# One scaled V copy, longer P and Z buffer rows and a remade order in a gated mix of softmax and linear attention

## The chip, the core and the metric

The kernel runs on 1 core of one Trainium2 chip. The metric is the device time of one execution in microseconds, the median over the runs; lower is better. Engines are called by their names: TensorE (PE in the profile), VectorE (DVE), ScalarE (ACT), GpSimd (POOL) and SyncE (SP, which issues the DMAs).

## The reference

Both attentions work on the same `x` (2048 rows of 512, bf16) with 32 heads of 16 columns. The result is a gated mix of the two.

```python
def _A_ref(x, wqkv, wo):                      # softmax attention
    ...                                       # q, k, v: 32 heads of 16
    scores = jnp.einsum("bhqd,bhkd->bhqk", q, k) * (Dh ** -0.5)
    p = _softmax(scores, axis=-1)
    o = jnp.einsum("bhqk,bhkd->bhqd", p, v)
    return o.transpose(0, 2, 1, 3).reshape(B, S, D) @ wo

def _B_ref(x, wqkv, wo):                      # linear attention
    phi = lambda t: jnp.where(t > 0, t + 1, jnp.exp(t)) + 1e-6
    pq, pk = phi(q), phi(k)
    kv = jnp.einsum("bhsd,bhse->bhde", pk, v)
    z = jnp.einsum("bhsd->bhd", pk)
    num = jnp.einsum("bhqd,bhde->bhqe", pq, kv)
    den = jnp.einsum("bhqd,bhd->bhq", pq, z)[..., None] + 1e-6
    return (num / den).transpose(0, 2, 1, 3).reshape(B, S, D) @ wo

g = _sigmoid((x * gate_w).sum(-1, keepdims=True))
return g * _A_ref(x, A_wqkv, A_wo) + (1 - g) * _B_ref(x, B_wqkv, B_wo)
```

## The kernel before

**Units.** The softmax attention is cut into 2048 units: one head, 128 keys (a key block), 512 queries (a query chunk). The 32 heads are taken as four groups `t8` of eight heads; in a round, four heads (one parity of a group) are at work at once, one on each quarter of the TensorE array. There are 32 rounds of 64 units. The scores of a unit are one matmul of `Qz` and `KT` (`ps<-Qz,KT`), written to one of eight PSUM banks.

**Two ways to an exponential.** Pairs of units go to ScalarE, which takes the exponential of two banks in one instruction (`P<-ps`, 128x1024, L1141) and writes two of the `NP` P buffers. The other units go to VectorE, which computes the exponential by its bits: it adds a constant and writes an integer that, read as bf16, is a piecewise linear power of two (`Z<-ps`, L1089 for one unit, L1053 for a pair). GpSimd then adds two integer constants (`SHIFTS`) to it (`INT64_ADD`, L1115), which gives two more such terms. The sum of the `NTERM` = 3 terms, with weights `WTS`, follows the power of two closely. The three results fill three of the `NZ` Z buffers, each of which holds two units.

**Product with V.** The weights aren't applied to the terms: each term is multiplied by a V that carries its weight. `Vp` holds V with a column of ones (for the softmax's sum); `Vs` holds V times the weight, made by VectorE in `t_vs` (L1420) from `Vp`, for two groups of heads at a time. So a unit of ScalarE brings one matmul (`ps<-P,Vp`), and a unit of VectorE three (`ps<-Z,Vp` for the first term, `ps<-Z,Vs` for the others). Four such matmuls, of four heads, run side by side and add up in the round's accumulating bank. The last two rounds have them cut in halves of 256 queries. When a round is done VectorE transposes and normalises it.

**All other work** is spread between the units as tasks: the projections to K, Q and V, the linear attention (phi, its K-V product, its denominators), the gate and the last projection with the output rows (`t_final`, L1645 writes an output row block to one of two `outt` buffers, from which a DMA takes it to memory). A task takes a PSUM bank, has its matmuls, and frees the bank after VectorE or ScalarE has read it.

**What sets the order.** The program holds a planner that runs when the kernel is built. It keeps a clock for each engine with a cost for each instruction, always picks the engine that can start first, and there the candidate with the best start and priority: scores (`cand_s`), VectorE's first term (`cand_op1`), shifts (`cand_shift`), ScalarE's exponentials (`cand_exp`), products with V (`cand_pv`) and the tasks. The streams that it lays out are fixed; on the chip each engine runs its own stream and waits on semaphores. How many units go to VectorE comes out of that: `cand_s` builds a step of scores with two banks for ScalarE and, where banks are free and

```python
zok = len(z_free()) >= z_need() + NTERM and len(full) < X("DMX")
```

holds, one or two for VectorE. The planner's thresholds `X(...)` are read from a table `PLAN`, by the number of units issued so far divided by 8, with `DEF` for what an entry leaves out.

Of the kernel before, what the change touches and what calls it, by code (L numbers as in the profile page):

```python
# [8 lines left out]
ALU = mybir.AluOpType  # L9
# [136 lines left out]
def bass_gated_mix__mha_block__linear_attn_block__prompt_kernel(  # L146
# [19 lines left out]
    SHIFTS = (0, 42, 85)  # L166
    WTS = (1.0, 0.79296875, 0.63671875)

    def spl(t):
# [277 lines left out]
    with ExitStack() as es:  # L447
# [36 lines left out]
        OAT = SB([128, NT8, S], BF16, "OAT")  # L484
# [519 lines left out]
        def v_res(t8, w, kb):  # L1004
            return r_Vp[t8][kb // 2] if w == 0 else r_Vs[t8 % 2][w - 1][kb // 4]
# [943 lines left out]
```

## Time and profile before

| | |
|---|---|
| median of 3 runs | 625.99 us |
| lowest, highest | 625.38, 626.42 us |
| span of the profiled execution | 624.3 us |
| the profiled execution's own time | not listed apart from its span |
| busy: TensorE, VectorE, ScalarE, GpSimd | 616.6, 596.5, 610.2, 470.5 us |
| granted TensorE clock | 1.000 |

The span goes from the first to the last instruction. Busy time counts an instruction from its start to the end of its record; records of one engine overlap by some tens of nanoseconds or more, so that the time which one of them occupies is better read from start to start in the timeline. In the groups by line, L639 is a helper through which nearly all matmuls go; there the names of the operands tell the work apart.

### The profile page before, as it was taken

How to read it: one execution, taken by the hardware profiler on the slowest of the kernel's cores; microseconds unless marked ns; L12 is line 12 of the kernel's file. 1: busy time of each engine (PE TensorE's matmuls, PEld its weight loads, DVE VectorE, ACT ScalarE, POOL GpSimd, SP SyncE). 2: the span in 40 equal slices, each digit the busy share in tenths (PEclk: the TensorE clock that was granted, in tenths of full speed). 3: DMA queues.
4: the chain of work that ended last, by engine and by line, in shares of the span. 5: the costliest groups of instructions: out<-in, count | busy, mean ns of one | idle time of the engine just before them, and what ended most of it. 6: DMA issues, size and time to landing. Idle time of an engine off the chain costs nothing.

```text
span 624.3 us, 19695 instructions
## 1 busy us (share of the span) xinstructions
PE 616.6 (99%) x8432; PEld 188.9 (30%) x8432; DVE 596.5 (96%) x941; ACT 610.2 (98%) x682; POOL 470.5 (75%) x802
## 2 busy tenths in 40 slices
PE   8999999999999999999999999999999999999997
PEld 5432322433222232332222222222222222222343
DVE  6999999999999999999999999999999999999995
ACT  5999999999999999999999999999999999999996
POOL 3577687677687889866867687767799788987893
PEclk9999999999999999999999999999999999999999
DMA  6711003001110010111101011121100102010101
GB/s 145 200 43 22 14 1 54 2 2 28 36 25 4 9 27 3 19 44 26 51 8 23 26 41 24 38 50 52 28 9 17 29 11 35 3 18 27 19 11 36
DMA packets 68367, 19.64 MB, mean 31 GB/s; under 512 B 56500, under 2 KB 68148, under 8 KB 68280
## 3 DMA queue, kind: packets, MB, share of 16 engines
q1 hardware_dynamic: 67464, 17.99, 13.3%
q8 instruction: 66, 1.08, 0.7%
q10 hardware_dynamic: 816, 0.39, 0.2%
q14 instruction: 21, 0.17, 0.1%
HBM read 8.92 MB, written 4.46 MB: 21 GB/s over the span
## 4 chain that ended last, share of the span: by engine, by line
ACT 78%; PE 21%; issue 0%; POOL 0%; POOLq 0%
ACT P L1141 76%; PE ps L639 20%; ACT eb L1495 2%; PE ps L1288 0%; PE ps L1344 0%; ACT P L1643 0%; POOL warm L709 0%; ACT KT L1320 0%; POOLq L1934 0%
## 5 line engine op out<-in xcount | busy, mean ns | idle before, releaser
L1141 ACT ACTIVATE P<-ps 128x1024 bf16<-128x1024 f32 x642 | 597.4, 1138 | 3.0 <-PE ps L639 2.8
L1115 POOL INT64_ADD Z<-Z x784 | 465.3, 611 | 142.6 <-DVE Z L1089 103.9
L1089 DVE TENSOR_SCALAR Z<-ps 128x512 int16<-128x512 f32 x534 | 348.2, 680 | 11.0 <-PE ps L639 8.8
L639 PE MATMUL ps<-Qz,KT 32*128 32x512 bf16 x2048 | 255.4, 384 | 3.1 <-ACT P L1141 1.6
L639 PE MATMUL ps<-Z,Vs 128*17 128x512 bf16 (+1 forms) x1620 | 249.6, 370 | 0.1
L639 PE MATMUL ps<-P,Vp 128*17 128x512 bf16 (+1 forms) x1366 | 236.6, 369 | 0.0
L639 PE MATMUL ps<-Z,Vp 128*17 128x512 bf16 (+1 forms) x810 | 188.4, 370 | 0.0
L1053 DVE TENSOR_SCALAR Z<-ps 128x1024 int16<-128x1024 f32 x115 | 139.8, 1216 | 3.4 <-PE ps L639 1.4
L639 PEld LDWEIGHTS ps<-Qz,KT 32*128 32x128 bf16 x2048 | 66.3, 90 | 249.7 <-ACT P L1141 210.3
L639 PEld LDWEIGHTS ps<-Z,Vs 128*17 128x17 bf16 x1620 | 59.0, 89 | 47.5 <-issue 34.9
L639 PEld LDWEIGHTS ps<-P,Vp 128*17 128x17 bf16 x1366 | 54.9, 89 | 51.8 <-issue 47.1
L639 PEld LDWEIGHTS ps<-Z,Vp 128*17 128x17 bf16 x810 | 44.7, 88 | 21.8 <-issue 15.2
L639 PE MATMUL ps<-xT,wA 128*32 128x512 bf16 (+2 forms) x560 | 37.5, 369 | 0.0
L1448 DVE STREAM_TRANSPOSE T<-ps 128x512 f32<-128x512 f32 x32 | 22.6, 707 | 3.4 <-PE ps L639 3.4
L1495 ACT ACTIVATE eb<-ps 128x512 bf16<-128x512 f32 x32 | 22.3, 698 | 0.0
L1497 DVE SCALAR_TENSOR_TENSOR phiK<-ps,eb 128x512 bf16<-128x512 f32 x32 | 21.8, 680 | 0.2
L639 PE MATMUL ps<-wB,OAT 128*32 128x512 bf16 x256 | 20.4, 384 | 0.0
L639 PE MATMUL ps<-wA,xT 128*32 128x256 bf16 x512 | 20.1, 275 | 0.0
L639 PE MATMUL ps<-wB,phiK 128*32 128x512 bf16 x256 | 19.3, 382 | 0.0
L639 PE MATMUL ps<-phiK,xnat 128*32 128x512 bf16 x256 | 18.6, 383 | 0.0
L639 PE MATMUL ps<-xT,wB 128*32 128x512 bf16 x256 | 17.8, 382 | 0.0
L639 PE MATMUL ps<-wB,xT 128*32 128x512 bf16 x256 | 17.4, 381 | 0.0
(81 smaller groups left out, 193.2 us busy)
## 6 DMA issues: line engine op xcount, KB each, us to landing
xnat<-rcpd SPq DMA_DIRECT2D x16, 128.0 KB
Qz<-QT SPq DMA_DIRECT2D x120, 16.0 KB, 1.8
oad<-T SPq DMA_DIRECT2D x60, 32.0 KB, 1.9
out_dram<-outt SPq DMA_DIRECT2D x14, 128.0 KB, 1.8
wB<-in_B_wqkv_dram SPq DMA_DIRECT2D x3, 512.0 KB, 5.8
wA<-in_A_wqkv_dram SPq DMA_DIRECT2D x11, 128.0 KB, 3.3
xnat<-in_A_x_dram SPq DMA_DIRECT2D x2, 512.0 KB, 8.2
xnat<-in_A_x_dram SPq DMA_DIRECT2D x6, 128.0 KB, 2.6
```

The costliest lines, as they stand in the source:

```text
L639: return lambda: nc.tensor.matmul(o, lhsT=l, rhs=r, start=start, stop=stop, skip_group_check=True)
L1053: res.append(C(DV, 400, 1131, lambda: nc.vector.tensor_scalar(Z[:, zs[0], :], bank(b2[0], 2), ZB, 0.0, op0=ALU.add, op1=ALU.max), [r_bank[ ...
L1089: res.append(C(DV, prio, 598, lambda: nc.vector.tensor_scalar(Z[:, z, 512 * h:512 * (h + 1)], bank(b), ZB, 0.0, op0=ALU.add, op1=ALU.max), ...
L1115: return C(PO, 300, 160 + 0.4165 * (hi - lo), lambda: nc.gpsimd.int64_add(Z[:, zw, lo:hi].bitcast(I64), Z[:, z0, lo:hi].bitcast(I64), cst) ...
L1141: return C(AC, 500, 426.5 * n + 51, lambda: nc.scalar.activation(P[:, slot:slot + n, :].rearrange("p a b -> p (a b)"), bank(bs[0], n), ACT ...
L1448: yield dv(623, lambda: nc.vector.transpose(T1[:, par, :], bank(b)), [r_bank[b]], [r_T1[par]])
L1495: yield ac(477, lambda: nc.scalar.activation(e16, bank(b), ACT.Exp), [r_bank[b]], [r_eb[i]])
L1497: yield dv(598, lambda: nc.vector.scalar_tensor_tensor(dst_ap, bank(b), 1.0 + 1e-6, e16, op0=ALU.add, op1=ALU.max), [r_bank[b], r_eb[i]], ...
```

## The change

- `WTS` becomes (1.0, 1.0, 0.75) and `SHIFTS` (0, 41, 87). The second term's weight is 1, so it uses `Vp`. `SCALED` lists the terms that still need a scaled copy, only the third; `t_vs` makes one copy in place of two, and `Vs` is half as large.
- `NP` goes from 20 to 24 and `NZ` from 18 to 21.
- An output row block takes whichever of the two `outt` buffers is free, in place of the one of its own parity; it no longer waits for the row block two before it.
- `PLAN` has other values throughout (254 entries in place of 257), so the planner lays out other streams.

```diff
-    SHIFTS = (0, 42, 85)
-    WTS = (1.0, 0.79296875, 0.63671875)
+    SHIFTS = (0, 41, 87)
+    WTS = (1.0, 1.0, 0.75)
+    SCALED = [w for w in range(len(WTS)) if WTS[w] != 1.0]
...
-    NP, NZ, NQZ = 20, 18, 3
+    NP, NZ, NQZ = 24, 21, 3
...
     PLAN = {
...
-        Vs = SB([128, 2, NTERM - 1, NKB * 8, 18], BF16, "Vs")
+        Vs = SB([128, 2, len(SCALED), NKB * 8, 18], BF16, "Vs")
...
         def v_ap(t8, w, kb, h):
             i = 8 * kb + h
-            return Vp[:, t8, i, 0:17] if w == 0 else Vs[:, t8 % 2, w - 1, i, 0:17]
+            return Vp[:, t8, i, 0:17] if w not in SCALED else Vs[:, t8 % 2, SCALED.index(w), i, 0:17]
 
         def v_ok(t8, w, kb):
-            return ("p", t8, kb // 2) in V_ready if w == 0 else ("s", t8, kb // 4) in V_ready
+            return ("p", t8, kb // 2) in V_ready if w not in SCALED else ("s", t8, kb // 4) in V_ready
...
-            for w in range(1, NTERM):
-                yield dl(_Port(216, 84), lambda w=w: nc.vector.tensor_scalar(Vs[:, t8 % 2, w - 1, sl, :], Vp[:, t8, sl, :], WTS[w], None, op0=ALU.mult),
-                         [r_Vp[t8][2 * vb], r_Vp[t8][2 * vb + 1]], [r_Vs[t8 % 2][w - 1][vb]])
+            for i, w in enumerate(SCALED):
+                yield dl(_Port(216, 84), lambda i=i, w=w: nc.vector.tensor_scalar(Vs[:, t8 % 2, i, sl, :], Vp[:, t8, sl, :], WTS[w], None, op0=ALU.mult),
+                         [r_Vp[t8][2 * vb], r_Vp[t8][2 * vb + 1]], [r_Vs[t8 % 2][i][vb]])
...
-            o = qb % 2
-            ot, ro = outt[:, o, :], [r_outt[o]]
             dst = out2[128 * qb:128 * (qb + 1), :]
             if tail:
-                ot, ro = P[:, 2 * qbl, :], [r_P[2 * qbl]]
+                o, ot, ro = qb % 2, P[:, 2 * qbl, :], [r_P[2 * qbl]]
             else:
-                yield ("WAIT", lambda: qb < 2 or ("f", qb - 2) in flags)
+                yield ("WAIT", lambda: not all(st["obusy"]))
+                o = st["obusy"].index(False)
+                st["obusy"][o] = True
+                ot, ro = outt[:, o, :], [r_outt[o]]
...
             yield ("DMA", dst, ot, semOUT[o], out_fill[o], 2200.0, ro, [], False, True)
-            yield ("FLAG", lambda: flags.add(("f", qb)))
+            if not tail:
+                st["obusy"][o] = False
```

More of the change, by code (lines that the diff above doesn't have):

```diff
@@ new lines, in bass_gated_mix__mha_block__linear_attn_block__prompt_kernel @@
+        0: {"SKEW": 0, "PWN": 200, "RIDE": 600, "UEX": -0.3, "REL": 0.5, "PORT": 1, "SGL": 410, "JIT": 3, "O1P": 440, "RSV": 400, "DMX": 2},
+        1: {"SKEW": 0, "DSL": 0, "DTOL": 250, "PWT": 250, "PWN": 200, "HD": 60, "SLK": -100, "UEX": -0.3, "REL": 0.5, "SGL": 410, "TST": 900, "O1P": 440, "ACP": 450, "SWP": 1, "EAR": 300, "O1W": 300, "DMX": 2},
+        2: {"SKEW": 0, "DSL": 0, "DTOL": 250, "PWT": 250, "PWN": 200, "HD": 300, "SLK": -100, "UEX": -0.3, "REL": 0.5, "SGL": 410, "TST": 900, "O1P": 440, "ACP": 450, "SWP": 1, "EAR": 300, "O1W": 300, "DMX": 2},
@@ new lines, in bass_gated_mix__mha_block__linear_attn_block__prompt_kernel @@
+        18: {"SKEW": 0, "DSL": 150, "DTOL": 250, "PWN": 100, "HD": 300, "SLK": -100, "UEX": -0.3, "REL": 1, "SGL": 410, "TST": 900, "O1P": 440, "ACP": 450, "EAR": 300, "TMX": 2, "DMX": 2},
+        19: {"SKEW": 0, "DSL": 150, "DTOL": 250, "PWN": 100, "HD": 300, "SLK": -100, "UEX": -0.3, "REL": 1, "SGL": 410, "TST": 900, "O1P": 440, "ACP": 450, "EAR": 300, "TMX": 2, "DMX": 2},
+        20: {"SKEW": 0, "DSL": 300, "DTOL": 1000, "PWE": 50, "PWT": 250, "PWN": 200, "TPR": 720, "RIDE": 1800, "UEX": -0.3, "REL": 1, "SGL": 410, "TST": 610, "PRE": 150, "O1P": 440, "DMX": 4, "NAJ": 1},
@@ new lines, in bass_gated_mix__mha_block__linear_attn_block__prompt_kernel @@
+        29: {"SKEW": 6, "DSL": 0, "DTOL": 5000, "PWT": 250, "PWN": 100, "TPR": 450, "RIDE": 2500, "HP": 220, "HD": 60, "SLK": -100, "TOP": 800, "ROOM": 4, "PORT": 1, "SGL": 395, "TST": 610, "O1P": 410, "EAR": 300, "TMX": 2, "NAJ": 1},
+        30: {"PWT": 250, "HP": 160, "ROOM": 1, "ACP": 450},
+        31: {"SKEW": 0, "DSL": 300, "DTOL": 1000, "PWE": 50, "PWT": 250, "PWN": 200, "TPR": 720, "RIDE": 1800, "UEX": -0.3, "REL": 1, "SGL": 410, "TST": 610, "O1P": 440, "TMX": 2, "DMX": 4, "NAJ": 1},
+        32: {"SKEW": 0, "DSL": 300, "DTOL": 1000, "PWE": 50, "PWT": 250, "PWN": 200, "TPR": 720, "RIDE": 1800, "UEX": -0.3, "REL": 1, "SGL": 410, "TST": 610, "O1P": 440, "TMX": 2, "DMX": 4, "NAJ": 1},
@@ new lines, in bass_gated_mix__mha_block__linear_attn_block__prompt_kernel @@
+        44: {"SKEW": 3, "DSL": 300, "DTOL": 2000, "PWE": 200, "PWT": 250, "TPR": 650, "RIDE": 300, "HP": 160, "HD": 0, "SLK": -100, "UEX": -0.3, "ROOM": 4, "REL": 1, "PORT": 1, "SGL": 395, "TST": 900, "O1P": 440, "RSV": 400, "TMX": 2, "O1W": 300, "DMX": 4, "NAJ": 1},
+        46: {"DSL": 150, "DTOL": 1000, "PWE": 50, "PWN": 100, "TPR": 650, "RIDE": 1800, "HD": 60, "SLK": -100, "ROOM": 4, "REL": 0.5, "PORT": 1, "SGL": 410, "TST": 900, "O1P": 440, "SWP": 1, "EAR": 900, "RSV": 400, "NAJ": 1},
+        47: {"SKEW": 0, "EAR": 300},
@@ new lines, in bass_gated_mix__mha_block__linear_attn_block__prompt_kernel @@
+        50: {"DSL": 150, "DTOL": 1000, "PWE": 200, "PWN": 100, "TPR": 650, "RIDE": 1800, "HD": 60, "NDB": 1, "SLK": -100, "UEX": 0.6, "ROOM": 1, "REL": 0.5, "PORT": 1, "SGL": 410, "TST": 900, "O1P": 440, "SWP": 1, "EAR": 900, "RSV": 400, "TMX": 2},
+        51: {"DSL": 150, "DTOL": 1000, "PWE": 200, "PWN": 100, "TPR": 650, "RIDE": 1800, "HD": 60, "NDB": 1, "SLK": -100, "UEX": 0.6, "ROOM": 1, "REL": 0.5, "PORT": 1, "SGL": 410, "TST": 900, "O1P": 440, "SWP": 1, "EAR": 900, "RSV": 400, "TMX": 2},
@@ new lines, in bass_gated_mix__mha_block__linear_attn_block__prompt_kernel @@
+        89: {"TPR": 720, "HP": 160},
+        90: {"SKEW": 0, "DSL": 300, "DTOL": 250, "PWE": 50, "PWT": 250, "PWN": 100, "TPR": 560, "RIDE": 1800, "HD": 0, "UEX": -0.3, "REL": 1, "SGL": 395, "TST": 610, "O1P": 440, "SWP": 1, "TMX": 2, "NAJ": 1},
+        92: {"SKEW": 3, "DSL": 300, "DTOL": 2000, "PWE": 50, "TPR": 450, "HP": 160, "HD": 0, "SLK": -100, "UEX": -0.3, "REL": 1, "PORT": 1, "SGL": 395, "TST": 900, "PRE": 0, "ACP": 450, "SWP": 1, "EAR": 0, "RSV": 200, "DMX": 4, "NAJ": 1},
+        93: {"SKEW": 0, "DSL": 300, "DTOL": 250, "PWE": 50, "PWT": 250, "PWN": 200, "TPR": 560, "RIDE": 1800, "HD": 0, "UEX": -0.3, "REL": 1, "SGL": 395, "TST": 610, "O1P": 440, "SWP": 1, "TMX": 2, "NAJ": 1},
@@ new lines, in bass_gated_mix__mha_block__linear_attn_block__prompt_kernel @@
+        94: {"SKEW": 2, "DSL": 300, "DTOL": 250, "PWE": 50, "PWT": 250, "PWN": 200, "TPR": 560, "RIDE": 1800, "HD": 0, "REL": 1, "SGL": 395, "TST": 610, "PRE": 150, "SWP": 1, "TMX": 2, "NAJ": 1},
+        95: {"SKEW": 0, "DSL": 300, "DTOL": 0, "PWE": 50, "PWT": 250, "PWN": 100, "TPR": 560, "RIDE": 1800, "HD": 0, "UEX": -0.3, "REL": 1, "PORT": 1, "SGL": 395, "TST": 610, "O1P": 440, "SWP": 1, "NAJ": 1},
+        96: {"SKEW": 2, "DSL": 300, "DTOL": 250, "PWE": 50, "PWT": 400, "PWN": 200, "TPR": 560, "RIDE": 1800, "HP": 220, "HD": 0, "SGL": 395, "TST": 610, "PRE": 0, "TMX": 2, "NAJ": 1},
@@ new lines, in bass_gated_mix__mha_block__linear_attn_block__prompt_kernel @@
+        100: {"SGL": 395, "PRE": 150},
+        101: {"SGL": 395, "PRE": 150},
+        102: {"SKEW": 2, "DSL": 300, "DTOL": 2000, "PWE": 50, "PWT": 250, "TPR": 560, "HP": 160, "HD": 0, "SLK": -100, "UEX": -0.3, "REL": 1, "PORT": 1, "SGL": 395, "TST": 900, "PRE": 0, "O1P": 440, "ACP": 450, "SWP": 1, "EAR": 150, "RSV": 400, "NAJ": 1},
+        103: {"SKEW": 2, "DSL": 300, "DTOL": 2000, "PWE": 50, "PWT": 250, "TPR": 720, "HP": 160, "HD": 0, "SLK": -100, "UEX": -0.3, "REL": 1, "PORT": 1, "SGL": 395, "TST": 900, "PRE": 0, "O1P": 440, "ACP": 450, "SWP": 1, "EAR": 150, "RSV": 400, "O1W": 300, "NAJ": 1},
@@ new lines, in bass_gated_mix__mha_block__linear_attn_block__prompt_kernel @@
+        114: {"SKEW": 2, "DTOL": 250, "PWE": 50, "PWT": 100, "HD": 60, "SLK": -100, "UEX": -0.3, "TOP": 800, "SGL": 410, "TST": 900, "PRE": 150, "O1P": 440, "ACP": 450, "SWP": 1, "DMX": 2, "NAJ": 1},
+        115: {"HP": 160},
+        116: {"DSL": 150, "DTOL": 1000, "PWE": 50, "PWT": 400, "TPR": 650, "RIDE": 1800, "HD": 60, "SLK": -100, "ROOM": 4, "REL": 0.5, "PORT": 1, "SGL": 410, "TST": 900, "O1P": 440, "SWP": 1, "EAR": 900, "RSV": 400, "NAJ": 1},
+        117: {"DSL": 150, "DTOL": 1000, "PWE": 50, "PWT": 400, "TPR": 650, "RIDE": 1800, "HD": 60, "SLK": -100, "ROOM": 4, "REL": 0.5, "PORT": 1, "SGL": 410, "TST": 900, "O1P": 440, "SWP": 1, "EAR": 900, "RSV": 400, "NAJ": 1},
@@ new lines, in bass_gated_mix__mha_block__linear_attn_block__prompt_kernel @@
+        155: {"SLK": 0},
+        156: {"SKEW": 3, "DSL": 40, "DTOL": 0, "PWT": 250, "RIDE": 300, "HP": 160, "HD": 0, "SLK": 0, "UEX": -0.3, "ROOM": 4, "PORT": 1, "SGL": 395, "TST": 900, "PRE": 300, "O1P": 440, "SWP": 1, "EAR": 300, "RSV": 400, "DMX": 4, "NAJ": 1},
+        157: {"SKEW": 3, "DSL": 40, "DTOL": 0, "PWT": 250, "RIDE": 300, "HP": 160, "HD": 0, "SLK": 0, "UEX": -0.3, "ROOM": 4, "PORT": 1, "SGL": 395, "TST": 900, "PRE": 300, "O1P": 440, "SWP": 1, "EAR": 300, "RSV": 400, "DMX": 4, "NAJ": 1},
@@ new lines, in bass_gated_mix__mha_block__linear_attn_block__prompt_kernel @@
+        213: {"SKEW": 3, "DSL": 40, "DTOL": 2000, "PWT": 250, "HD": 0, "SLK": -100, "UEX": -0.3, "ROOM": 4, "REL": 0.5, "PORT": 1, "SGL": 395, "TST": 900, "PRE": 300, "O1P": 440, "SWP": -1, "EAR": 300, "RSV": 400, "O1W": 300, "DMX": 4, "NAJ": 1},
+        214: {"SKEW": 6, "DSL": 0, "DTOL": 5000, "PWN": 100, "TPR": 560, "RIDE": 2500, "HD": 60, "SLK": -100, "TOP": 800, "ROOM": 4, "PORT": 1, "SGL": 395, "TST": 610, "O1P": 410, "EAR": 300, "TMX": 2, "NAJ": 1},
+        215: {"DSL": 150},
+        216: {"DSL": 150, "DTOL": 1000, "PWE": 50, "PWT": 400, "TPR": 650, "RIDE": 1800, "HD": 60, "SLK": -100, "ROOM": 2, "REL": 0.5, "PORT": 1, "SGL": 410, "TST": 900, "O1P": 440, "EAR": 900, "RSV": 400, "NAJ": 1},
@@ L535, in bass_gated_mix__mha_block__linear_attn_block__prompt_kernel @@
         r_Vp = [[R(f"V{p}_{t}") for t in range(8)] for p in range(NT8)]
-        r_Vs = [[[R(f"V{p}_{w}_{t}") for t in range(NQC)] for w in range(NTERM - 1)] for p in range(2)]
+        r_Vs = [[[R(f"V{p}_{w}_{t}") for t in range(NQC)] for w in SCALED] for p in range(2)]
         r_P = [R(f"P{i}") for i in range(NP)]
@@ L753, in bass_gated_mix__mha_block__linear_attn_block__prompt_kernel @@
         phi_free = [True, True]
-        st = {"tail": False, "boot": True, "pv_round": 0, "s_done": False, "acc_free": True, "mode": "full", "ab": 7, "pvr": [0] * 4, "dopen": None, "useq": 0}
+        st = {"tail": False, "boot": True, "pv_round": 0, "s_done": False, "acc_free": True, "mode": "full", "ab": 7, "pvr": [0] * 4, "dopen": None, "useq": 0, "obusy": [False, False]}
         pieces_left = [4 * NKB] * NR
@@ L1004, in v_res @@
         def v_res(t8, w, kb):
-            return r_Vp[t8][kb // 2] if w == 0 else r_Vs[t8 % 2][w - 1][kb // 4]
+            return r_Vp[t8][kb // 2] if w not in SCALED else r_Vs[t8 % 2][SCALED.index(w)][kb // 4]
         def v_ap(t8, w, kb, h):
             i = 8 * kb + h
-            return Vp[:, t8, i, 0:17] if w == 0 else Vs[:, t8 % 2, w - 1, i, 0:17]
+            return Vp[:, t8, i, 0:17] if w not in SCALED else Vs[:, t8 % 2, SCALED.index(w), i, 0:17]
         def v_ok(t8, w, kb):
-            return ("p", t8, kb // 2) in V_ready if w == 0 else ("s", t8, kb // 4) in V_ready
+            return ("p", t8, kb // 2) in V_ready if w not in SCALED else ("s", t8, kb // 4) in V_ready
         def add_piece(u, w, ap, res, rel):
```

474 lines of the change are left out of this document (217 added, 257 removed).

## The prediction

> **What bounds the kernel now.** I read the page first: the busy times, the slices, the chain of work that ended last. Then the groups by line, then the timelines of ScalarE, VectorE and TensorE.
>
> ```profile
> span 624.3 us, 19695 instructions
> PE 616.6 (99%) x8432; PEld 188.9 (30%) x8432; DVE 596.5 (96%) x941; ACT 610.2 (98%) x682; POOL 470.5 (75%) x802
> ACT 78%; PE 21%; issue 0%; POOL 0%; POOLq 0%
> ```
>
> Three engines look full. The chain says which one sets the end: 78% of it is ScalarE. The groups by line say what each engine does (count, busy time, mean of one, idle time before it):
>
> ```profile
> L1141 ACT ACTIVATE P<-ps 128x1024 bf16<-128x1024 f32 x642 | 597.4, 1138 | 3.0 <-PE ps L639 2.8
> L1115 POOL INT64_ADD Z<-Z x784 | 465.3, 611 | 142.6 <-DVE Z L1089 103.9 <-DVE Z L1053 34.0 <-DVE Zbd L1531 0.8
> L1089 DVE TENSOR_SCALAR Z<-ps 128x512 int16<-128x512 f32 x534 | 348.2, 680 | 11.0 <-PE ps L639 8.8
> L639 PE MATMUL ps<-Z,Vs 128*17 128x512 bf16 (+1 forms) x1620 | 249.6, 370 | 0.1
> L639 PE MATMUL ps<-Z,Vp 128*17 128x512 bf16 (+1 forms) x810 | 188.4, 370 | 0.0
> L1053 DVE TENSOR_SCALAR Z<-ps 128x1024 int16<-128x1024 f32 x115 | 139.8, 1216 | 3.4 <-PE ps L639 1.4
> L1420 DVE TENSOR_SCALAR Vs<-Vp 128x576 bf16<-128x576 bf16 x32 | 10.1, 336 | 0.0
> L1645 DVE TENSOR_SCALAR outt<-ps,gg 128x512 bf16<-128x512 f32 x14 | 10.4, 744 | 0.4 <-PE ps L639 0.4
> ```
>
> A unit is 128 keys by 512 queries of one head. ScalarE takes 642 x 2 = 1284 of them; VectorE takes 534 + 2 x 115 = 764; together 2048, which is the whole softmax. So every pair of units that VectorE takes saves ScalarE one exponential. The timeline of ScalarE shows that nothing else could set the end (start, length, count, idle time before):
>
> ```profile
> 8.20 1.94 ACT L1141 ACTIVATE P<-ps 128x1024 bf16<-128x1024 f32 x2 [0.34 <-PE ps L639]
> ...
> 22.15 24.14 ACT L1141 ACTIVATE P<-ps 128x1024 bf16<-128x1024 f32 x26 [1.25 <-PE ps L639]
> ...
> 163.51 113.33 ACT L1141 ACTIVATE P<-ps 128x1024 bf16<-128x1024 f32 x123 [0.23 <-PE ps L639]
> ...
> 411.83 205.93 ACT L1141 ACTIVATE P<-ps 128x1024 bf16<-128x1024 f32 x224
> 621.26 0.69 ACT L1643 ACTIVATE P<-ps,gg 128x512 bf16<-128x512 f32 x1 [3.51 <-PE ps L639]
> ```
>
> From 22.15 us to 411.83 + 205.93 = 617.8 us ScalarE waits once, for 0.23 us. One exponential costs (205.93 - 1.14) / 223 = 0.918 us from start to start, so 0.459 us a unit. The 6.5 us behind 617.8 are the last output rows, which the change leaves as they are. The time is therefore: the start, plus 0.918 us times the number of exponentials, plus fixed ScalarE work, plus a fixed tail. **What the change is worth is how many units it moves from ScalarE to VectorE**, and VectorE has to have the time for them.
>
> The profiled execution has a span of 624.3 us; the median of the runs shown is 625.99, 1.7 us more, which I take as lying outside the span and unchanged. I work out a difference and take it off 625.99.
>
> **The change, part by part.** *One scaled V copy.* `t_vs` issues one multiplication in place of two, for 4 groups of V times 4 quarters: 16 of the 32 L1420 instructions go. What one occupies is read from start to start, as records overlap:
>
> ```profile
> 27.32 0.30 DVE L1420 TENSOR_SCALAR Vs<-Vp 128x576 bf16<-128x576 bf16 x1
> 27.54 1.40 DVE L1089 TENSOR_SCALAR Z<-ps 128x512 int16<-128x512 f32 x2
> ...
> 41.61 2.47 DVE L1089 TENSOR_SCALAR Z<-ps 128x512 int16<-128x512 f32 x4
> 44.03 0.69 DVE L1389 TENSOR_SCALAR QT<-ps 128x512 bf16<-128x512 f32 x1
> ...
> 46.48 0.95 DVE L1420 TENSOR_SCALAR Vs<-Vp 128x576 bf16<-128x576 bf16 x2
> 47.36 0.68 DVE L1089 TENSOR_SCALAR Z<-ps 128x512 int16<-128x512 f32 x1
> ```
>
> One takes 0.22 us, or 0.44 in the pair at 46.48. I take 0.26, near the low end, because the group's mean record of 0.336 is close to the lone 0.30 and far from the slow ones. That frees 16 x 0.26 = 4.1 us of VectorE (ends 3.5 and 7.0). Freed time is not saved time: it must be filled with units. One unit costs VectorE (44.03 - 41.61) / 4 = 0.605 us, and the end moves forward by 0.459 us for it, which VectorE loses too. So u units fit where u x (0.605 + 0.459) = 4.1, u = 3.9, and the end comes 3.9 x 0.459 = 1.8 us earlier (ends 1.5 and 3.0; 0 if the order doesn't use it).
>
> On TensorE the second term's matmuls change from Vs to Vp; both groups have a mean of 370 ns, so nothing. Each unit moved brings two more column matmuls, a quarter of a four-wide step each; GpSimd gets one more shift per unit, 0.61 us, against 142.6 us in which it waits.
>
> *21 Z and 24 P buffers.* A unit on VectorE holds three half Z buffers until its three products with V are done, and `cand_s` sends VectorE a new unit only while three buffers beyond the need of the waiting ones are free. How full they are, from Z's instructions up to two moments (stretch, length, then busy time and count of TensorE's matmuls, weight loads, VectorE, GpSimd; units go in with three pieces each, TensorE's count is pieces out):
>
> ```profile
> 0.00:332.50 332.50, 138.74 (x1130) 30.38 (x1130) 244.36 (x343) 234.94 (x396) 1.00 0.17 36
> 0.00:485.00 485.00, 215.04 (x1742) 47.69 (x1742) 366.10 (x506) 355.66 (x599) 1.00 0.16 34
> ```
>
> Of the 343 and 506 VectorE instructions, 44 and 79 carry two units by L1053's rows:
>
> ```profile
> 0.00:332.50 332.50, 53.61 (x44) 1.00 0.17 36
> 0.00:485.00 485.00, 96.06 (x79) 1.00 0.16 34
> ```
>
> At 332.5 us that is 3 x 387 - 1130 = 31 halves, 15.5 of 18 buffers; at 485 us 3 x 585 - 1742 = 13 halves, 6.5 of 18. So the limit is met in some places and far off in others. What there is to win is VectorE's idle time:
>
> ```profile
> 20.00:600.00 580.00, 565.13 (x877) 1.00 0.13 28
> ```
>
> And how it waits, in the timeline:
>
> ```profile
> 487.57 0.39 PE L639 MATMUL ps<-Qz,KT 32*128 32x512 bf16 x3
> ...
> 488.01 0.69 DVE L1089 TENSOR_SCALAR Z<-ps 128x512 int16<-128x512 f32 x1 [0.39 <-PE ps L639]
> ...
> 488.44 0.39 PE L639 MATMUL ps<-Qz,KT 32*128 32x512 bf16 x3
> ...
> 488.88 0.69 DVE L1089 TENSOR_SCALAR Z<-ps 128x512 int16<-128x512 f32 x1 [0.18 <-PE ps L639]
> ```
>
> Between 20 and 600 us it is 580 - 565.1 = 14.9 us. All of it filled would give 14.9 / 1.064 = 14 units, 6.4 us; none, 0. I take a third, 5.0 us, 4.7 units, 2.1 us, because only part of the idle time lies where Z is full: at 488 us, right behind the moment with 6.5 of 18 in use, VectorE waits for scores that come three at a time (two for ScalarE, one for it), and buffers don't cure that. P has no price: ScalarE waits 0.23 us from 22.15 us on, so full P buffers never stop it; the gain is 0 to 0.2 us.
>
> *Any free output row buffer.* VectorE waits 0.4 us in all before the 14 L1645 copies: 0 to 0.4 us of VectorE, 0.2 us of the end; I take 0. Two buffers stay two, so behind a copy that waits for a row's transfer the same VectorE queue stands as before.
>
> *The order.* All engines' streams are laid out anew. The start holds ScalarE idle for 0.34 us at 8.20 up to 1.25 us at 22.15: a new order can win or lose about 2 us there. I take 0.
>
> Sum: -1.8 - 2.1 = -3.9 us; 8.6 units, about 638 exponentials in place of 642. 625.99 - 3.9 = **622.1 us**.
>
> **The rivals.** *All of VectorE's idle time is filled.* For it: the waits at 488 us repeat, and in the fuller stretch Z is at 15.5 of 18. Against: 6.5 of 18 at 485 us. It gives -1.8 - 6.4 = -8.2, 617.8 us. The Trainium skill, Perfetto Trace Analysis, section Optimization Strategy, says that the same gap repeating on an engine that should be saturated can mean too few SBUF or PSUM buffers for the next tile. By that rule the longer Z row would fill these gaps; the two Z counts agree with it at one place of the two. 0.18.
>
> *The time freed stays idle.* VectorE has one multiplication less, but the order gives it no more units: the number of exponentials stays 642 and the time 626.0. For it: scores come from TensorE, which is the releaser of 8.8 of 11.0 us of L1089's idle time. Against: one unit more every 70 us is little to find. 0.12.
>
> *Slower: scores come late for ScalarE behind long TensorE bursts.* Place: the projections. Price:
>
> ```profile
> 163.65 1.05 PE L639 MATMUL ps<-phiK,xnat 128*32 128x512 bf16 x16
> 164.63 0.39 PE L639 MATMUL ps<-Qz,KT 32*128 32x512 bf16 x3
> ```
>
> A burst of 16 holds TensorE for 0.98 us, longer than an exponential of 0.918; around it stands the only hole behind the start, 0.23 us. Deeper P and Z rows let an order put off products with V and run more such bursts. 3.9 / 0.23 = 17 such holes eat the whole gain, so from there it decides; 26 of them give -3.9 + 6.0 = +2.1, 628.1 us. Against: TensorE is given 8.6 x 2 / 4 = 4.3 four-wide steps more, under 1 us over the whole kernel, and there was one hole in 595 us. 0.18.
>
> **How the numbers follow.** The forecast, 622.1 with an own range of 620 to 624.5, has the remaining 0.52. About 0.2% (1.25 us) is what a measurement of this kernel can tell from no change. Faster by more: 0.52 + 0.18 = 0.70; within: 0.12; slower: 0.18. The range goes from the first rival's 617.8 to the slower one's 628.1.
>
> **What would show it.** Right: L1420 at 16; the Z,Vs and Z,Vp matmul counts changed round (about 820 and 1640); L1141 at 636 to 640 with 0.918 us each; L1089 and L1053 together at 768 to 776 units; ScalarE without holes behind 22 us; VectorE's idle time from 20 to 600 us near 10 us. Wrong: L1141 still at 642, which is the second rival; idle time of ScalarE before L1141 of several us with TensorE as releaser, which is the slower one; or a ScalarE start or tail that moved by over 2 us, which no term here holds.

## The result, and the profile after

| | before | changed |
|---|---|---|
| median | 625.95 us | 621.36 us |
| lowest, highest | 625.38, 626.42 | 621.03, 621.53 |
| span of the profiled execution | 624.3 | 619.6 |

The ratio is 0.9927, interval 0.9913 to 0.9942: 4.6 us faster. The forecast was 622.1 us, in a range of 617.8 to 628.1.

The groups by line of the changed kernel (line numbers are two lower than before):

```profile
L1139 ACT ACTIVATE P<-ps 128x1024 bf16<-128x1024 f32 x637 | 594.2, 1128 | 2.8 <-PE ps L637 2.3
L1087 DVE TENSOR_SCALAR Z<-ps 128x512 int16<-128x512 f32 x518 | 337.4, 679 | 8.7 <-PE ps L637 6.9
L637 PE MATMUL ps<-Z,Vp 128*17 128x512 bf16 (+1 forms) x1644 | 250.6, 369 | 0.2 <-DVE T L1446 0.2
L637 PE MATMUL ps<-Z,Vs 128*17 128x512 bf16 (+1 forms) x822 | 177.2, 369 | 0.0
L1051 DVE TENSOR_SCALAR Z<-ps 128x1024 int16<-128x1024 f32 x128 | 155.4, 1214 | 4.2 <-PE ps L637 3.1
L1418 DVE TENSOR_SCALAR Vs<-Vp 128x576 bf16<-128x576 bf16 x16 | 5.5, 343 | 0.0
```

VectorE now takes 518 + 2 x 128 = 774 units in place of 764, ScalarE 637 exponentials in place of 642. The timeline of ScalarE:

```profile
24.14 28.63 ACT L1139 ACTIVATE P<-ps 128x1024 bf16<-128x1024 f32 x31 [0.27 <-PE ps L637]
...
265.74 6.52 ACT L1139 ACTIVATE P<-ps 128x1024 bf16<-128x1024 f32 x7 [0.18 <-PE ps L637]
272.54 24.99 ACT L1139 ACTIVATE P<-ps 128x1024 bf16<-128x1024 f32 x27 [0.28 <-PE ps L637]
...
408.77 204.27 ACT L1139 ACTIVATE P<-ps 128x1024 bf16<-128x1024 f32 x222
616.57 0.69 ACT L1642 ACTIVATE P<-ps,gg 128x512 bf16<-128x512 f32 x1 [3.52 <-PE ps L637]
```

The last exponential ends at 408.77 + 204.27 = 613.0 us, 4.7 us earlier; the tail behind it is 6.6 us, as long as before. One exponential is (204.27 - 1.13) / 221 = 0.919 us from start to start in the mean, as before. Five of them fewer are 4.6 us at that mean, which is the whole result.

VectorE between 20 and 600 us, and Z's instructions up to 248 us with the paired ones among them:

```profile
20.00:600.00 580.00, 567.97 (x866) 1.00 0.13 28
...
0.00:248.00 248.00, 101.53 (x864) 21.83 (x864) 186.18 (x257) 179.58 (x303) 1.00 0.18 39
...
0.00:248.00 248.00, 51.08 (x43) 1.00 0.18 39
```

VectorE's idle time fell from 14.9 to 12.0 us. At 248 us, 3 x 300 - 864 = 36 half buffers are held: 18 whole ones, all that the row before had. The order does use the longer row, but seldom: counted in this way all through the traces, the order before never holds more than 33 halves, and the changed one holds more than 33 for 1% of its span.

One line of the page changed more than the time did, the chain that ended last:

```profile
PE 51%; ACT 39%; DVE 9%; issue 0%; POOL 0%; POOLq 0%
```

Before, it was 78% ScalarE. The experiments had to say whether that means another bound.

### The profile page after: what moved, and what is told of

Read it like the earlier page. It is cut to its first block, busy times and chain, and to the rows that moved or that the text cites. A ratio compares the mean times of both kernels' runs of the same rounds, so it can differ in the third digit from the quotient of the medians.

```text
span 619.6 us, 19711 instructions
## 1 busy us (share of the span) xinstructions
PE 611.0 (99%) x8448; PEld 185.7 (30%) x8448; DVE 594.6 (96%) x922; ACT 605.9 (98%) x677; POOL 474.6 (77%) x812
## 4 chain that ended last, share of the span: by engine, by line
PE 51%; ACT 39%; DVE 9%; issue 0%; POOL 0%; POOLq 0%
PE ps L637 50%; ACT P L1139 38%; DVE Z L1087 5%; DVE phiK L1495 1%; DVE Z L1051 1%; ACT eb L1493 1%; DVE eb L1494 0%; DVE KT L1371 0%; DVE T L1446 0%; PE ps L1286 0%; DVE phiK L1604 0%; DVE xnat L1585 0%; PE ps L1342 0%; DVE Qz L1302 0%; DVE Vs L1418 0%
## 5 line engine op out<-in xcount | busy, mean ns | idle before, releaser
L1139 ACT ACTIVATE P<-ps 128x1024 bf16<-128x1024 f32 x637 | 594.2, 1128 | 2.8 <-PE ps L637 2.3
L1087 DVE TENSOR_SCALAR Z<-ps 128x512 int16<-128x512 f32 x518 | 337.4, 679 | 8.7 <-PE ps L637 6.9
L637 PE MATMUL ps<-Z,Vp 128*17 128x512 bf16 (+1 forms) x1644 | 250.6, 369 | 0.2 <-DVE T L1446 0.2
L637 PE MATMUL ps<-Z,Vs 128*17 128x512 bf16 (+1 forms) x822 | 177.2, 369 | 0.0
L1051 DVE TENSOR_SCALAR Z<-ps 128x1024 int16<-128x1024 f32 x128 | 155.4, 1214 | 4.2 <-PE ps L637 3.1
L637 PEld LDWEIGHTS ps<-Z,Vp 128*17 128x17 bf16 x1644 | 58.6, 89 | 36.9 <-issue 26.1
L637 PEld LDWEIGHTS ps<-Z,Vs 128*17 128x17 bf16 x822 | 41.9, 89 | 28.9 <-issue 22.9
```

Of the source, the lines that this page charges most:

```text
L637: return lambda: nc.tensor.matmul(o, lhsT=l, rhs=r, start=start, stop=stop, skip_group_check=True)
L1051: res.append(C(DV, 400, 1131, lambda: nc.vector.tensor_scalar(Z[:, zs[0], :], bank(b2[0], 2), ZB, 0.0, op0=ALU.add, op1=ALU.max), [r_bank[ ...
L1087: res.append(C(DV, prio, 598, lambda: nc.vector.tensor_scalar(Z[:, z, 512 * h:512 * (h + 1)], bank(b), ZB, 0.0, op0=ALU.add, op1=ALU.max), ...
L1139: return C(AC, 500, 426.5 * n + 51, lambda: nc.scalar.activation(P[:, slot:slot + n, :].rearrange("p a b -> p (a b)"), bank(bs[0], n), ACT ...
```

## The experiments

Theory A is the prediction's: ScalarE's exponentials alone set the end, and the other engines' waits would take in some more work. The rivals are B, C, D, E and O, P, as they stand in the expectations. Nearly all kernels keep the order of the streams as it is and add or take away work on one engine, so that only that work differs. Behind each median stands its ratio to the kernel before, taken on the same chip. The difference given behind the ratio is this ratio times 625.95, against 621.36 (or against 625.95 for the two runs on the kernel before), so it can differ by some tenths from the difference of the medians.

**Relieve VectorE in the order before.**

```diff
             for w in range(1, NTERM):
+                cs = slice(32 * vb, 32 * vb + 1) if w == 1 else sl
-                ... nc.vector.tensor_scalar(Vs[:, t8 % 2, w - 1, sl, :], Vp[:, t8, sl, :], WTS[w], ...)
+                ... nc.vector.tensor_scalar(Vs[:, t8 % 2, w - 1, cs, :], Vp[:, t8, cs, :], WTS[w], ...)
...
-            return Vp[:, t8, i, 0:17] if w == 0 else Vs[...]
+            return Vp[:, t8, i, 0:17] if w < 2 else Vs[...]
```

> The kernel before in its own order, with the second term's scaled copies cut from 576 to 18 elements (16 instructions; the second term reads V itself, so its weight is left out). VectorE is relieved of about 16 x 0.2 = 3 us, and still gets 764 units. Theory A (ScalarE's 642 exponentials set the end, freed VectorE time is worth nothing until the order fills it): 626.0, within 0.6 us. Theory B (VectorE's time passes through to the end even in the same order): 623 to 624.

625.81 us, ratio 1.0003 (0.9995 to 1.0012). Its groups by line have the time gone from VectorE:

```profile
L1421 DVE TENSOR_SCALAR Vs<-Vp 128x18 bf16<-128x18 bf16 (+1 forms) x32 | 7.4, 255 | 0.0
```

10.1 us have become 7.4, and the end doesn't move. So a thinner copy is worth nothing in an order that stays as it is: time freed on VectorE reaches the end only where the order is remade to give VectorE more units.

**Add work to one engine in the changed order.** Each of these four puts some 5 us, or in one case more, on one engine, in up to 20 places.

```diff
-  lambda i=i, w=w: nc.vector.tensor_scalar(Vs[...], Vp[:, t8, sl, :], WTS[w], None, op0=ALU.mult)
+  [lambda i=i, w=w: ..., lambda: nc.vector.tensor_scalar(scr[:, 0:504]..., Vp[:, t8, 32 * vb:32 * vb + 28, :], 0.75, None, op0=ALU.mult)]
```

> The changed kernel in its own order, with a second scaled copy behind each of the 16 (504 elements, written to a spare tile that nobody reads): about 16 x 0.2 = 3.2 us more on VectorE. Theory A: VectorE's 12.0 us of waits between 20 and 600 us take it in, 621.4 to 622.0. Theory B: the work passes through, 624 to 625.

628.73 us, ratio 1.0048 (1.0036 to 1.0060): 7.6 us, over twice what even theory B expected. The group shows why, and the timeline where:

```profile
L1421 DVE TENSOR_SCALAR scr<-Vp 128x504 bf16<-128x504 bf16 x16 | 10.5, 657 | 0.0
```

```profile
20.65 0.28 DVE L1421 TENSOR_SCALAR scr<-Vp 128x504 bf16<-128x504 bf16 x1
...
44.86 1.23 DVE L1053 TENSOR_SCALAR Z<-ps 128x1024 int16<-128x1024 f32 x1
...
46.00 0.30 DVE L1420 TENSOR_SCALAR Vs<-Vp 128x576 bf16<-128x576 bf16 x1
...
46.19 1.23 POOL L1115 INT64_ADD Z<-Z  x2 [1.29 <-DVE Z L1053]
46.22 0.72 DVE L1421 TENSOR_SCALAR scr<-Vp 128x504 bf16<-128x504 bf16 x1
...
46.86 0.68 DVE L1089 TENSOR_SCALAR Z<-ps 128x512 int16<-128x512 f32 x1
```

Alone, the copy takes 0.28 us. At 46.22, 0.03 us behind the start of a shift on GpSimd, it takes 0.72 and ends 0.14 us behind the first of the two shifts (46.19 + 1.23 / 2 = 46.80). Of the 16, the two that meet no shift take 0.28 us; the other 14 start 0.03 to 0.11 us behind the start of a shift and take 0.69 to 0.72. The planner had put the first copy ahead of the shift; the second falls on it. The Trainium skill (SBUF — State Buffer, Who interferes with whom) says that a `tensor_scalar` in one of VectorE's two-port modes and a GpSimd instruction share a port pair, and that whichever issues first has it for its whole instruction while the other is blocked. This trace agrees: the copy behind the shift's start is held up until the shift is done. No run here shows separately that the copy is in such a mode. The work added was thus 16 x (0.66 - 0.08) = 9.2 us of VectorE (0.08 is the overlap of one record with the next), and 7.6 / 9.2 = 0.8 of it showed.

```diff
-  yield ac(477, lambda: nc.scalar.activation(e16, bank(b), ACT.Exp), ...)
+  two = nphi[0] % 7 in (1, 4)
+  yield ac(477, [lambda: nc.scalar.activation(e16, bank(b), ACT.Exp)] + [lambda: nc.scalar.activation(scr[:], bank(b), ACT.Exp)] * two, ...)
```

> The changed kernel in its own order, with 10 of the 32 exponentials of the linear attention taken twice (the second result goes to a spare tile): 10 x 0.49 = 4.9 us more on ScalarE. Theory A: all of it shows, 626.0 to 626.5. Theory B: all of it shows too, so this run tells A and B from a third one (C: TensorE alone sets the end, as 50% of the changed kernel's chain would suggest), by which under 1 us shows, 621.4 to 622.4.

626.16 us, ratio 1.0006 (0.9997 to 1.0015): 5.0 us for 4.9. Theory C, TensorE alone, is out.

```diff
             gs = proj4(b, ...)          # in all t_phik, and in one t_phiq of four
+            gs[0] = gs[0] * 2
```

> The changed kernel in its own order, with the first matmul step of 20 projections of the linear attention done twice: 80 matmuls, 20 steps of four side by side, 20 x 0.215 = 4.3 us more on TensorE. Theory A: TensorE's waits for ScalarE take in nearly all of it, 621.4 to 622.4. Theories B and C: it passes through, 625 to 625.7.

624.48 us, ratio 0.9976 (0.9966 to 0.9986): 3.1 us for 4.3. Theory A, which wanted 1.0 us at most, fails here.

```diff
-  lambda: nc.gpsimd.int64_add(Z[:, zw, lo:hi]..., Z[:, z0, lo:hi]..., cst)
+  [lambda: ...] + [lambda: nc.gpsimd.int64_add(scr[:]..., Z[:, z0, lo:lo + 512]..., cst)] * (issued[0] // 8 in POOLX and w == 1)
```

> The changed kernel in its own order, with 12 further shifts of half a Z buffer on GpSimd, in seven places spread over the kernel (results go to a spare tile): 12 x about 0.37 = 4.4 us more. GpSimd waits 134.5 us for VectorE, so by every theory 621.4, within 0.8 us. Over 623 would make GpSimd a fourth engine that the order leaves no slack.

623.02 us, ratio 0.9948 (0.9933 to 0.9963): 1.3 us for 12 x 0.396 = 4.8 us. That is more than the 0.8 us expected, by every theory, and a smaller share than on any other engine. ScalarE's timeline has a place for most of it, one late unit:

```profile
399.83 1.02 ACT L1144 ACTIVATE P<-ps 128x1024 bf16<-128x1024 f32 x1 [0.84 <-PE ps L640]
```

**VectorE again, without the port.** The run with two copies mixes work and port; here the added work reads PSUM.

```diff
-  yield dv(598, lambda: nc.vector.scalar_tensor_tensor(dst_ap, bank(b), ...), ...)
+  yield dv(598, [lambda: ...] + [lambda: nc.vector.tensor_copy(scr[:, 0:400], bank(b)[:, 0:400])] * two, ...)
```

> The changed kernel in its own order, with 10 further copies of 400 columns from PSUM on VectorE (to a spare tile): 10 x about 0.48 = 4.8 us, with no input from SBUF. Theory A as it stood (waits take it in): 621.4 to 622. Theory D (VectorE and TensorE are as full as ScalarE, so that about 0.8 of any time added to one shows, as the two runs before suggest): 624.5 to 626.

625.09 us, ratio 0.9977 (0.9968 to 0.9987): 3.1 us for 4.8. The same edit in the kernel before:

> The kernel before in its own order, with 10 further copies of 400 columns from PSUM on VectorE, 4.8 us, as in the run on the changed kernel that came out 3.7 us slower. If the order before leaves VectorE real room (14.9 us of waits between 20 and 600 us, ScalarE without holes): 626 to 627. If its order is as tight as the changed one's: 629 to 630.

628.61 us, ratio 1.0042 (1.0028 to 1.0055): 2.6 us for 4.8, between the two ranges that were expected. So the order before was nearly as tight, though its ScalarE had one visible hole behind 22 us. The groups of both runs tell where the time went (before with the extra work, then changed with it):

```profile
L1143 ACT ACTIVATE P<-ps 128x1024 bf16<-128x1024 f32 x642 | 597.9, 1112 | 3.5 <-PE ps L641 2.8
```

```profile
L1141 ACT ACTIVATE P<-ps 128x1024 bf16<-128x1024 f32 x637 | 593.8, 1098 | 4.6 <-PE ps L639 4.0
```

Idle time before the exponentials rose by only 0.5 and 1.8 us, less than the ends moved. But the mean record fell, from 1138 to 1112 and from 1128 to 1098 ns. A record of 1.13 us overlaps the next by 0.2 us, so an exponential can come up to 0.2 us late and still start inside the record before it: no idle time is listed. The starts in the trace of the kernel before show such a case, with TensorE's work ahead of it:

```profile
323.99 2.12 ACT L1141 ACTIVATE P<-ps 128x1024 bf16<-128x1024 f32 x2
...
324.89 1.21 ACT L1141 ACTIVATE P<-ps 128x1024 bf16<-128x1024 f32 x1
...
325.56 1.05 PE L639 MATMUL ps<-xT,wA 128*32 128x512 bf16 x16
...
325.80 2.21 ACT L1141 ACTIVATE P<-ps 128x1024 bf16<-128x1024 f32 x2
...
326.54 0.39 PE L639 MATMUL ps<-Qz,KT 32*128 32x512 bf16 x3
...
326.98 1.02 ACT L1141 ACTIVATE P<-ps 128x1024 bf16<-128x1024 f32 x1
```

The exponential at 324.89 starts 0.90 us behind the one before it; the one at 326.98 starts 1.18 us behind, when a burst of 16 projection matmuls has let its scores through; its record is 1.02 us long in place of 1.21. Of the exponentials that follow another in this trace, about 70% start 0.904 us behind it, within 4 ns; I take that as the step of one that has its scores. Behind 22 us, 62 start more than 0.94 us behind the one before, and the timeline lists one of them as a wait; in the changed kernel it is 67, and three are listed. Every one of these starts 0.02 us behind a semaphore update by TensorE.

Added up behind 22 us, the time from each exponential's start to ScalarE's next start exceeds 0.904 us by 9.9 us in the kernel before (7.1 of it at the 62 late ones) and by 12.5 with the extra work, by 11.0 in the changed kernel and 14.3 with it. These rises of 2.6 and 3.4 us are what the last exponential's end moved in the profiled executions (2.7 and 3.3). So the work added on VectorE reached the end as exponentials that started late, behind TensorE.

**Relieve ScalarE, then all three.**

```diff
-  nc.scalar.activation(e16, bank(b), ACT.Exp)
+  nc.scalar.activation(e16[:, 0:128], bank(b)[:, 0:128], ACT.Exp)     # the rest of phi reads these columns four times
```

> The changed kernel in its own order, with the 32 exponentials of the linear attention cut from 512 to 128 columns (the other columns take the first ones' values, so phi is left out in part): 32 x 0.32 = 10.2 us less on ScalarE, and some 3 us less on VectorE. Theory A (ScalarE alone sets the end): 611 to 612. Theory D (the three engines are equally full): no more than a third of it comes out, 618 to 621.

619.68 us, ratio 0.9898 (0.9881 to 0.9915): 1.8 us out of 10. Theory A, which wanted 611 to 612, is refuted. The exponentials now wait, and by their starts more than the idle time says: behind 22 us these exceed 0.904 us by 15.8 us, against 11.0 in the changed kernel:

```profile
L1139 ACT ACTIVATE P<-ps 128x1024 bf16<-128x1024 f32 x637 | 592.8, 1088 | 5.6 <-PE ps L637 4.2
```

```diff
+  (the edit above, and)
+  cs = slice(32 * vb, 32 * vb + 1)     # the 16 copies: 18 elements in place of 576
+  return Vp[:, t8, i, 0:17]            # in v_ap: the third term reads V itself, its weight is left out
+  gs[1] = []                           # one matmul step of four, in all t_phik and t_phiq
```

> The changed kernel in its own order, relieved on all three engines at once: the run with the 32 short exponentials (10.2 us less on ScalarE, some 3 us on VectorE), its scaled copies cut to 18 elements (2.9 us on VectorE), and one of the four matmul steps left out of the 32 projections of the linear attention (32 x 0.215 = 6.9 us less on TensorE). Theory D (three engines equally full): 615 to 617.5, clearly more than the 1.7 us of the ScalarE run alone. If something else holds the order (latencies between engines, PSUM banks), it stays near 619.7.

616.24 us, ratio 0.9842 (0.9828 to 0.9855): 5.3 us, three times the ScalarE run. Taking work from the other two as well lets more of ScalarE's relief come out. Theory D holds as far as that; but it is 5.3 of some 10 us on ScalarE, not all. TensorE wasn't relieved alone, so how much of the 5.3 us its part would give by itself is open.

**No copy at all.**

```diff
-    SHIFTS = (0, 41, 87)
-    WTS = (1.0, 1.0, 0.75)
+    SHIFTS, weights (0, 35, 83), (1.0, 1.0, 1.0)   # each term reads Vp; the 16 copies cut to 18 elements
```

> The changed kernel in its own order, one step further: all three weights 1, shifts (0, 35, 83), every term reads V itself, and the 16 scaled copies cut to 18 elements, so about 16 x 0.18 = 2.9 us less on VectorE. Theory A and D alike (freed time of one engine is worth nothing in a fixed order, since the other two stay as full): 621.4, within 0.7 us. Theory E (the changed kernel's order hangs on VectorE, as work added there shows nearly in full): 619 to 620.

621.41 us, ratio 0.9926 (0.9912 to 0.9939): nothing, as A and D had it; E is out. This is the step that would come next, and like the first one it would need an order of its own. None was made for it, so no version here beats the changed kernel with its work complete.

**The order, undone in two ways.** First the changed kernel with the table of before, then with its own table and the short rows.

```diff
-    PLAN = { ... 254 entries ... }
+    PLAN = { ... the 257 entries of before ... }
```

> The changed kernel (one copy, 24 P, 21 Z, any output buffer) with the table of the kernel before. Theory O (a table is fitted to one kernel, step by step, and is of no use to another): the streams then hold 669 exponentials in place of 637, so over 621.4 + 32 x 0.918 = 650.8. Theory P (the table's values are general and the copies and buffers carry the gain): 621 to 626.

657.96 us (a single run).

```diff
-    NP, NZ, NQZ = 24, 21, 3
+    NP, NZ, NQZ = 20, 18, 3
```

> The changed kernel with its own table, but 20 P and 18 Z buffers as before. The order is remade for them; its streams hold 670 exponentials in place of 637. Theory O (a table fits one kernel alone): over 621.4 + 33 x 0.918 = 651.7. If the longer rows were not used, the order would stay as it is and the time at 621.4.

662.16 us (a single run). The groups of both:

```profile
L1142 ACT ACTIVATE P<-ps 128x1024 bf16<-128x1024 f32 x669 | 624.5, 1103 | 7.6 <-PE ps L640 6.7
L1090 DVE TENSOR_SCALAR Z<-ps 128x512 int16<-128x512 f32 x515 | 339.4, 682 | 42.7 <-PE ps L640 39.4
```

```profile
L1139 ACT ACTIVATE P<-ps 128x1024 bf16<-128x1024 f32 x670 | 625.2, 1103 | 9.3 <-PE ps L637 8.4
L1087 DVE TENSOR_SCALAR Z<-ps 128x512 int16<-128x512 f32 x496 | 324.2, 683 | 40.1 <-PE ps L637 37.6
```

VectorE waits some 40 us for scores in both and takes fewer units. Theory O holds: a table is fitted to one kernel. My reading of the code is that with other buffers the steps fall elsewhere, and the thresholds for step 100 meet another state. These two runs therefore price an unfitted order, some 37 to 41 us, and not the buffers.

**The output rows.** With the old rule for the output buffers put back into the changed kernel, the planner lays out the same instructions in the same order on every engine; only the buffer that a row goes to, and the waits that belong to it, differ. So this part of the change moves no units. It was not run by itself.

## Why the prediction was right, and where not

- **The unit of account held.** 637 exponentials against about 638 forecast, 774 units on VectorE in a band of 768 to 776, 0.919 us each in the mean, the first exponential 0.25 us earlier and the tail as before: 5 x 0.918 = 4.6 us. The second rival (time left idle) didn't happen; the order filled it. The slower rival's sign didn't come either: the idle time before the exponentials is 2.8 us against 3.0, with three listed holes of 0.18 to 0.28 us from 24 us on, against one. By the starts, the excess over 0.904 us behind 22 us is 11.0 us against 9.9, so what this rival feared did happen, by 1.0 us.
- **The copy: 4.1 us of VectorE, right** (from start to start, all `Vs` copies take 8.6 us before and 4.5 after). **"0 if the order doesn't use it", shown** by the run that freed 2.7 us of records in the order before and got nothing.
- **The idle time and the price of a unit: two terms off, which offset by luck.** 5.0 us filled was too much: 14.9 - 12.0 = 2.9 us were. But the ten units cost far less than 0.605 us each: from start to start, idle time taken off, all of Z's VectorE instructions take 460.9 us before and 463.2 after, 2.3 us more. In part that is because 13 more instructions carry a pair of units, which the sum did not have. A pair takes 1.14 us from start to start (44.86 to 46.00 above), two singles 2 x 0.605 = 1.21, and 13 x 1.14 - 16 x 0.605 = 5.1 us. The rest is for the most part that the mean single fell from 0.618 to 0.613 us; why it fell isn't shown. With these, VectorE's balance closes: 4.1 from the copies, 2.9 from idle time, less 2.3 for the units, are the 4.7 us by which the kernel ends sooner.
- **The rule on gaps.** By the Trainium skill (Perfetto Trace Analysis, Optimization Strategy), gaps that repeat can mean too few buffers; the first rival had the longer row fill them all. A fifth of VectorE's idle time went, and for 1% of the span the row holds more than the order before ever held: here the rule bears out in small part at most.
- **What stays open.** Which share of the 4.6 us is due to the longer rows, which to the copy and which to the new table: the first two reach the time only through an order fitted to them, and no order was fitted to one of them alone. The old pair of copies beside the longer rows wasn't tried, and no new table was fitted to the kernel before, so a better table alone may hold a part of the gain.
- **What was wrong: "nothing else could set the end".** Work added to VectorE in the order before shows by 2.6 us of 4.8, and on TensorE and VectorE in the changed one by two thirds to four fifths. I read the single hole of 0.23 us as a ScalarE that never waits otherwise; by the starts, 62 exponentials came late behind 22 us, for 7.1 us in all, nearly all of it in waits that the timeline doesn't list. So the 0.918 us hold 0.904 us for an exponential that has its scores, and the rest is for the most part waiting. "P has no price" rests on the same premise; what the longer P row is worth was not measured. The sum came near because it asked how a planner shares units between two engines, which needs both to be nearly full, and that is what they are, with TensorE as the third. The chain's turn from 78% ScalarE to 51% TensorE is no change of the bound: among engines that wait for each other by tenths of a microsecond, the chain can run along any of them.

## What to carry to other kernels

Where several engines are full at once, count what is divisible between them and solve for the share. The time freed on one engine comes out at the end only after the order hands it new work. The factor is the unit's cost on the engine that gives it up over the sum of its costs on both, here 0.459 / 1.064 by the forecast's costs; it was more here, because the ten units cost VectorE less. Test fullness by adding a few microseconds to each engine in a fixed order, since neither busy shares nor the chain told TensorE, VectorE and ScalarE apart here, and taking work from VectorE or ScalarE alone gave between 0 and a fifth of it. Where records overlap, read waits from start to start: the idle time misses those shorter than the overlap. A table of thresholds that was fitted step by step belongs to one set of buffers: with others the loss, 37 and 41 us in two single runs, hides what the change is worth.

## What the runs showed of the hardware that I had not expected

A VectorE copy from SBUF to SBUF in bf16 (128x504) takes 0.28 us alone and 0.69 to 0.72 when it starts just behind a GpSimd shift; a mean of 0.657 over 16 of them. Copies that read PSUM (128x400) took 0.563 in the mean. So an edit that looks like 0.2 us on VectorE (the lone copy from start to start) can cost three times that (0.64) by where it falls, and the planner's placing of such copies is worth as much as the copies.

A ScalarE exponential of 128x1024 from PSUM starts 0.904 us behind the one before it when its scores are there. One that is late by up to some 0.2 us shows no idle time, only a later start and a record shorter than the 1.13 us of the mean, down to 1.02.
